# Placing every on-chip tile of a three-layer linear-attention kernel at a set distance modulo 128 bytes

## The chip, the core and the metric

The kernel runs on one core of a Trainium2 chip. The time is the device time of one execution in microseconds (us), the median of the runs named. The engines are TensorE (PE, its weight loads shown apart as PEld), VectorE (DVE), ScalarE (ACT), GpSimd (POOL) and SyncE (SP), which issues all DMAs here.

## What is computed

Three layers follow one another, for batch 8, 576 tokens, width 512 (8 heads of 64):

```python
# 1: linear attention, normalised per head
kv = einsum('bhsd,bhse->bhde', k, v)
o = einsum('bhsd,bhde->bhse', q, kv)
x = o / sqrt(mean(o*o, -1) + 1e-6) * g_norm        # heads put side by side: [B, S, 512]
# 2: gated layer
gate = sigmoid(sum_k conv_w[k] * shift(x, k))      # causal, 5 taps
x = (gate * (x @ w_val)) @ w_out
# 3: gMLP block
h = gelu_tanh(x @ w_in); u, v = h[..., :512], h[..., 512:]
v = layernorm(v) * g_ln
v = einsum('ts,bsd->btd', w_sg, v) + b_sg[:, None]
out = x + (u * v) @ w_out2
```

All inputs and the output are float32 in meaning; several weights arrive in a wider form and are converted on the chip.

## The kernel before, in words

**Products.** Every large product is done with three matmuls in the type fp32r: each operand is kept as a high part and a low part, and high x high, low x high and high x low are added in PSUM. `gemm3` (lines 212 to 220) does this for four K-tiles of 128, so it issues 12 matmuls; the stationary operand (`lhsT`, 128 x 128) changes with every matmul, the moving operand (`rhs`) has up to 512 columns. Each matmul has its own weight load, which the engine does beside the matmul before it.

**Stages, and which tile is stationary and which moving.**

- `o`, `kv`, `xT`: attention, in plain fp32 with small matmuls, and transposes.
- `val` (`Moe.val`, line 367): stationary `WV`, moving `X0h/X0l` or `X1h/X1l` (even or odd batch).
- `y` (`Moe.out`, line 388): stationary `WOh/WOl`, moving `Z`.
- `hv` (line 463, matmul in line 468): stationary `X1h/X1l`, moving `wiv`; for the last 64 tokens of two batches ("rest") the stationary tile is `kvbd0/kvbd1`.
- `hu` (line 513): stationary `wiu`, moving `X1h/X1l`. `hur` (line 561) is the same for the rest, with moving `XR`.
- `sg` (line 566, matmul in line 577): 14 matmuls of 288 columns for one piece; stationary the normalised v, which lies in `X0h`, `X0l`, `Q`, `K`, `V` and (rest) `X32`; moving the weight's high part in the tile `WV` and its low part in `G`.
- `out` (`wout2`, line 598): stationary `K/V` (which by then hold w_out2), moving `Z`; for the rest, moving `WOh`.

Of the products with 512 columns there are 384 matmuls each in `val`, `y`, `hu` and `out` and 432 in `hv`; `sg` has 896 with 288 columns; the rests have 96 with 256 columns for each of `val`, `y`, `hur` and `out`. Counts of the tags are those of the program.

**Order.** Batches 0 to 7 run through attention, `val` and `y` first, with attention of the next batch and the loading and splitting of the third layer's weights woven in by slot numbers (`Slots`, `later`, `tick`); then, batch by batch, `hu` and `sg`, then `hv` of the next batch and `out`. Intermediate results go to DRAM (`y_main`, `y_rest`) and come back. PSUM is one pool of 8 banks. The opening, up to the first `y`, is issued in an order written out by hand.

**Where tiles lie.** `sb(tag, shape)` (line 71) asks one pool for a tile. The pool lays out one place for each tag, in order of the first request, each as large as its largest user rounded up to 32 bytes per partition, behind a scratch of 16 KB for dynamic DMAs and 128 bytes of constants. A partition's tiles reach to 228,576 bytes of 229,376. All slices that the matmuls take out of a tile start at multiples of 128 bytes from its beginning (128 columns of 4 bytes are 512; 288 are 1152; 576 are 2304), so a tile's start modulo 128 bytes is that of each of its matmul operands. Worked out from the shapes, the starts modulo 128 are:

| tile | before | with the change |
|---|---|---|
| kvbd0, kvbd1 | 32 | 0 |
| WV | 64 | 0 |
| WOh, WOl | 64 | 32 |
| X32 | 64 | 0 |
| G | 0 | 0 |
| wiu | 96 | 96 |
| wiv | 96 | 64 |
| Y, Z, X0h, X0l, X1h, X1l | 96 | 0 |
| K, V | 96 | 64 |
| raw, Q, cv, T, XR | 96 | 0 |

The "distance" of a matmul is, in this document, the start of its stationary operand less the start of its moving operand, modulo 128:

| stage (columns) | stationary / moving before | distance | with the change | distance |
|---|---|---|---|---|
| val (512; rest 256) | 64 / 96 | 96 | 0 / 0 | 0 |
| y (512; rest 256) | 64 / 96 | 96 | 32 / 0 | 32 |
| hv (512) | 96 / 96 | 0 | 0 / 64 | 64 |
| hv, rest (512) | 32 / 96 | 64 | 0 / 64 | 64 |
| hu (512), hur (256) | 96 / 96 | 0 | 96 / 0 | 96 |
| out (512) | 96 / 96 | 0 | 64 / 0 | 64 |
| out, rest (256) | 96 / 64 | 32 | 64 / 32 | 32 |
| sg, X0 and Q (288) | 96 / 64 and 96 / 0 | 32 and 96 | 0 / 0 | 0 |
| sg, K and V (288) | 96 / 64 and 96 / 0 | 32 and 96 | 64 / 0 | 64 |
| sg, X32 (288) | 64 / 64 | 0 | 0 / 0 | 0 |

Of the kernel before, what the change touches and what calls it, by code (L numbers as in the profile page):

```python
# [19 lines left out]
P = 128  # L20
# [10 lines left out]
CG = math.sqrt(2.0 / math.pi)  # L31
AG = 0.044715
WC = 256

EXP_MAX = 1.875 * 2.0 ** -96
ELEMENTWISE = (mybir.EngineType.DVE, mybir.EngineType.Activation, mybir.EngineType.Pool)
# [25 lines left out]
def body(ctx, tc, qT, k, v, gcol, w_val, conv_w, w_out, w_in, g_ln, w_sgT, b_sg, w_out2, out, out_r):  # L62
    nc = tc.nc
    pool = ctx.enter_context(tc.tile_pool(name="sb", bufs=1))
# [4 lines left out]
    count = [0]  # L69

    def sb(tag, shape, dtype=F32, bufs=1):
        count[0] += 1
        return pool.tile([P] + shape, dtype, tag=tag, name=f"{tag}_{count[0]}", bufs=bufs)

    def tmp(n):

        return sb("T", [S], bufs=7)[:, :n]
# [16 lines left out]


    ident = sb("ident", [P])
    make_identity(nc, ident)
    signed = sb("GR", [2, P], F32R)
    for i, x in enumerate((1.0, -1.0)):
        nc.gpsimd.tensor_scalar(signed[:, i], ident, x, 0.0, op0=ALU.mult, op1=ALU.add)  # L100
# [34 lines left out]
    def split(src, h, l, raw=None, tmp=None, k=None, last=nc.gpsimd.tensor_tensor):  # L135
# [10 lines left out]
        def load():  # L146
            r = raw
            if r is None:
                r = sb("raw", [WC * 2], I32 if wide else F32, bufs=2)
            if not wide:  # L150
# [53 lines left out]
    def split_weight(w, src, c0, n):  # L204

        return [split(src[kt * P:(kt + 1) * P, c0 + c:c0 + c + WC], w[:, 0, kt, c:c + WC], w[:, 1, kt, c:c + WC])
                for c in range(0, n, WC) for kt in range(NK)]

# [218 lines left out]
    def w2_pieces():  # L427
        p2["kv"] = [sb(i, [5, D], F32R) for i in "KV"]
        p2["w2"] = w2 = [t[:, :NK] for t in p2["kv"]]
        return [split(w_out2[kt * P:(kt + 1) * P, c:c + WC], w2[0][:, kt, c:c + WC], w2[1][:, kt, c:c + WC])  # L430
                for c in range(0, D, WC) for kt in range(NK)]

# [230 lines left out]
    def taps():  # L663
        if conv_w.dtype == F32:
            dma(cw, conv_w)
            return lambda: None
        raw = sb("raw", [WC * 2], I32, bufs=2)[:, :2 * NK * KC]
        dma(raw, conv_w.bitcast(I32))
# [291 lines left out]
```

## Time and profile before

| what | us |
|---|---|
| median of 3 runs | 734.62 |
| lowest and highest of them | 734.25, 738.93 |
| profiled execution: span from its first to its last instruction | 733.0 |
| PE busy in it | 719.4 (98%) |
| PEld busy | 623.3 (85%) |
| DVE busy | 583.9 (80%) |
| ACT, POOL busy | 350.4 (48%), 153.3 (21%) |

The span is shorter than the median by 1.6 us, which lie around the instructions or between two executions. A matmul's recorded duration holds its whole way through the array, and consecutive matmuls overlap; what one costs in a stream is the time from its start to the start of the next, and the chain of waits shows that directly: a piece of it such as "2.72 ... x12" is 12 matmuls in a row that took 2.72 us from the first start to what follows.

### The profile page before, as it was taken

Reading aid. Unit: us, or ns where it says so; the run is one execution under the profiler, and the core shown is the slowest. Engines: PE = TensorE matmul, PEld = TensorE weight load, DVE = VectorE, ACT = ScalarE, POOL = GpSimd, SP = SyncE. Lnnn points to the kernel's source line nnn. Section 1 sums busy time; section 2 is a strip of 40 time slices with the busy share of each in tenths; the row PEclk is TensorE's granted clock in tenths of the full one; section 3 lists DMA queues with packets and bytes.
Section 4 is the critical chain, followed back from the end, with each engine's and each line's share of the span. In section 5 each row is a group of like instructions: output and inputs, shape, how many; then the busy total and the mean of one; then the engine's idle time right before and its main releaser. Section 6 shows DMA issues by size and latency. Waiting matters only on the chain.

```text
span 733.0 us, 11757 instructions
## 1 busy us (share of the span) xinstructions
PE 719.4 (98%) x4490; PEld 623.3 (85%) x4490; DVE 583.9 (80%) x1127; ACT 350.4 (48%) x667; POOL 153.3 (21%) x173
## 2 busy tenths in 40 slices
PE   8897999999999999999999999999999999999998
PEld 7686888888888888899889889888899888898897
DVE  6699979899979899699976877866866867867762
ACT  4666475566565575465533434424433424334230
POOL 1405337261627271212010000000100000100000
PEclk9999999999999999999999999999999999999999
DMA  9945253625363202533211221122240122111302
GB/s 307 352 140 202 73 193 130 223 80 195 111 223 134 87 15 86 201 97 121 68 72 58 87 101 30 58 87 59 87 158 29 59 87 62 63 63 44 101 1 86
DMA packets 56712, 81.19 MB, mean 111 GB/s; under 512 B 3664, under 2 KB 29264, under 8 KB 55632
## 3 DMA queue, kind: packets, MB, share of 16 engines
q1 hardware_dynamic: 56656, 80.45, 32.4%
q8 instruction: 35, 0.57, 0.3%
q14 instruction: 21, 0.17, 0.1%
HBM read 61.56 MB, written 18.87 MB: 110 GB/s over the span
## 4 chain that ended last, share of the span: by engine, by line
PE 86%; DVE 7%; issue 1%; POOL 1%; ACT 0%; DVEq 0%; POOLq 0%
PE sg L577 16%; PE hv L468 13%; PE out L218 13%; PE hu L218 12%; PE y L218 12%; PE val L218 11%; DVE G L349 4%; PE o L286 3%; PE xT L315 2%; PE kv L270 2%; PE hur L218 2%; DVE st L295 1%; DVE Z L381 0%; ACT Y L395 0%; DVE T L300 0%
## 5 line engine op out<-in xcount | busy, mean ns | idle before, releaser
L349 DVE SCALAR_TENSOR_TENSOR G<-X,cw,G 128x576 f32<-128x576 f32 x128 | 99.4, 826 | 6.1 <-ACT G L343 6.1
L218 PE MATMUL y<-Z,WOh 128*128 128x512 f32 (+1 forms) x320 | 98.9, 381 | 0.0
L480 POOL TENSOR_TENSOR bmv<-bmv,mhalf 128x1 f32<-128x1 f32 x36 | 21.5, 598 | 344.0 <-DVE bmv L479 344.0
L468 PE MATMUL hv<-wiv,X1h 128*128 128x512 f32 x256 | 83.1, 390 | 0.0
L218 PE MATMUL out<-Z,K 128*128 128x512 f32 x256 | 83.1, 389 | 0.0
L218 PE MATMUL hu<-X1h,wiu 128*128 128x512 f32 x256 | 79.4, 391 | 0.0
L297 POOL TENSOR_TENSOR st<-st,mhalf 128x8 f32<-128x8 f32 x40 | 70.5, 1769 | 7.4 <-DVE st L296 5.1
L218 PEld LDWEIGHTS y<-Z,WOh 128*128 128x128 f32 x320 | 57.8, 188 | 10.5
L457 ACT ACTIVATE T<-T 128x512 f32<-128x512 f32 x68 | 42.9, 631 | 44.8 <-DVE T L454 44.8
L218 PE MATMUL y<-Z,WOl 128*128 128x512 f32 (+1 forms) x160 | 58.9, 372 | 0.0
L218 PEld LDWEIGHTS out<-Z,K 128*128 128x128 f32 x256 | 48.1, 188 | 10.0
L468 PEld LDWEIGHTS hv<-wiv,X1h 128*128 128x128 f32 x256 | 47.7, 188 | 9.6 <-ACT X1h L445 0.2
L578 DVE SCALAR_TENSOR_TENSOR T<-sg,gln,WOl 128x288 f32<-128x288 f32 x64 | 32.8, 516 | 26.4 <-PE sg L577 26.2
L218 PEld LDWEIGHTS hu<-X1h,wiu 128*128 128x128 f32 x256 | 46.6, 188 | 8.3
L218 PE MATMUL hu<-X1l,wiu 128*128 128x512 f32 x128 | 50.0, 391 | 0.0
L468 PE MATMUL hv<-wiv,X1l 128*128 128x512 f32 x128 | 49.9, 390 | 0.0
L218 PE MATMUL out<-Z,V 128*128 128x512 f32 x128 | 49.8, 389 | 0.0
L589 ACT ACTIVATE Z<-T 128x512 fp32r<-128x512 f32 x32 | 20.1, 630 | 57.3 <-DVE T L588 57.3
L286 PEld LDWEIGHTS o<-kvbd,Q 128*128 128x128 f32 x320 | 40.3, 191 | 3.2 <-issue 0.7
L218 PE MATMUL val<-X0h,WV 128*128 128x512 f32 x128 | 41.4, 404 | 0.0
L286 PE MATMUL o<-kvbd,Q 128*128 128x128 f32 x320 | 40.7, 275 | 0.5 <-DMA Q<-in_qT_dram 0.5
L218 PE MATMUL val<-X1h,WV 128*128 128x512 f32 x128 | 41.2, 403 | 0.0
(174 smaller groups left out, 1709.0 us busy)
## 6 DMA issues: line engine op xcount, KB each, us to landing
Q<-in_qT_dram SPq DMA_DIRECT2D x8, 1152.0 KB, 6.0
y_main<-Y SPq DMA_DIRECT2D x8, 1024.0 KB, 3.9
raw<-y_main SPq DMA_DIRECT2D x32, 256.0 KB, 3.2
Y<-y_main SPq DMA_DIRECT2D x32, 256.0 KB, 3.9
out_dram<-Y SPq DMA_DIRECT2D x32, 256.0 KB, 2.3
K<-in_k_dram SPq DMA_DIRECT2D x7, 1024.0 KB, 5.7
V<-in_v_dram SPq DMA_DIRECT2D x7, 1024.0 KB, 9.1
raw<-in_w_in_dram SPq DMA_DIRECT2D x16, 256.0 KB, 4.7
```

The costliest lines, as they stand in the source:

```text
L218: nc.tensor.matmul(ps, lhsT=a[:, kt, msl], rhs=x[:, kt], start=(i == 0), stop=(i == 3 * NK - 1))
L270: nc.tensor.matmul(self.pk[j][h, h], lhsT=self.k[:, t, js][:, h], rhs=self.v[:, t, js][:, h], start=(t == 0), stop=(t == 4))
L286: nc.tensor.matmul(po[:, j * P:(j + 1) * P], lhsT=self.q[:, j, o:o + P], rhs=bd[:, j, :], start=True, stop=True)
L297: nc.gpsimd.tensor_tensor(st[:, 2], st[:, 1], mhalf, op=ALU.pow)
L315: nc.tensor.transpose(pt[:, j * P:(j + 1) * P], xo[:, j * P:(j + 1) * P], ident)
L349: stt(gate[:, m], x32[:, m, j:j + S], cw3[:, m, j:j + 1], gate[:, m], op0=ALU.mult, op1=ALU.add)
L457: act(w, w, AF.Tanh, scale=CG * AG)
L468: nc.tensor.matmul(ps, lhsT=a[:, kt], rhs=p2["wiv"][:, w, kt], start=(i == 0), stop=(i == 3 * NK - 1))
L480: nc.gpsimd.tensor_tensor(mv[:, 3:4], mv[:, 2:3], mhalf[:, 0:1], op=ALU.pow)
L577: nc.tensor.matmul(ps, lhsT=a[:, msl], rhs=w, start=(n == 0), stop=(n == len(mm) - 1))
L578: later(0, lambda: stt(vs[:, sl], ps, gln_s[:, m:m + 1], p2["bsg"][:, sl], op0=ALU.mult, op1=ALU.add))
L589: act(g[:, 0], x, AF.Copy)
```

## The change

Each tile's room is rounded up to 128 bytes per partition (32 words), and behind eight tags a stated number of words more is left free, which moves everything that lies behind them. The tile is asked for as a flat run of words with that padded shape and then viewed in its own shape. To have room, the scratch of the dynamic DMAs is set to 1 KB; the kernel issues all its DMAs from SP, none from POOL. With it the tiles reach to 214,656 bytes. No instruction, loop or slot is written otherwise.

```diff
+LINE = 32
+BEHIND = {"WV": 8, "WOl": -8 % LINE, "st": 0, "G": 24, "wiu": 24, "wiv": 16, "X1l": 16, "V": 16}
+
     def sb(tag, shape, dtype=F32, bufs=1):
         count[0] += 1
-        return pool.tile([P] + shape, dtype, tag=tag, name=f"{tag}_{count[0]}", bufs=bufs)
+        words = math.prod(shape)
+        room = -(-words // LINE) * LINE + BEHIND.get(tag, 0)
+        t = pool.tile([P, words], dtype, tag=tag, name=f"{tag}_{count[0]}", bufs=bufs, padded_shape=[P, room])
+        if len(shape) == 1:
+            return t
+        d = [f"d{i}" for i in range(len(shape))]
+        return t.rearrange(f"p ({' '.join(d)}) -> p {' '.join(d)}", **dict(zip(d, shape)))
...
-    nc = bacc.Bacc("TRN2", target_bir_lowering=False, num_devices=1)
+    nc = bacc.Bacc("TRN2", target_bir_lowering=False, num_devices=1, dynamic_dma_scratch_size=1024)
```

## Rows read from the trace of the kernel before

**Rows 1.** The page: busy time by engine, and the chain by line.

```profile
PE 719.4 (98%) x4490; PEld 623.3 (85%) x4490; DVE 583.9 (80%) x1127; ACT 350.4 (48%) x667; POOL 153.3 (21%) x173
...
PE sg L577 16%; PE hv L468 13%; PE out L218 13%; PE hu L218 12%; PE y L218 12%; PE val L218 11%; DVE G L349 4%; PE o L286 3%; PE xT L315 2%; PE kv L270 2%; PE hur L218 2%; DVE st L295 1%; DVE Z L381 0%; ACT Y L395 0%; DVE T L300 0%
```

**Rows 2.** Stretches: length, busy time (instructions) of each engine, granted clock, DMA share, GB/s.

```profile
core 0: us, PE busy (x) PEld busy (x) DVE busy (x) ACT busy (x) POOL busy (x), PEclk, DMA share, GB/s
0.00:18.00 18.00, 15.72 (x144) 14.28 (x146) 11.65 (x25) 8.73 (x14) 2.71 (x13) 1.00 0.92 307
18.00:30.00 12.00, 10.72 (x92) 8.65 (x87) 6.58 (x19) 6.17 (x16) 5.47 (x5) 1.00 1.02 350
30.00:66.00 36.00, 30.52 (x307) 25.30 (x305) 32.99 (x53) 24.32 (x45) 14.79 (x14) 1.00 0.69 237
66.00:333.00 267.00, 266.04 (x1777) 224.73 (x1778) 243.70 (x437) 163.31 (x315) 109.02 (x106) 1.00 0.37 129
333.00:733.00 400.00, 396.38 (x2181) 350.34 (x2179) 289.00 (x596) 147.90 (x279) 21.35 (x37) 1.00 0.22 71
```

**Rows 3.** Chain of waits in order of time, second layer: start, length, what.

```profile
133.88 1.09 ACT Y L395 x2
135.40 0.75 POOL cv L176
136.60 4.38 DVE G L349 x6
...
274.35 5.59 PE y L218 x24
279.94 11.20 PE val L218 x48
...
318.92 5.13 PE y L218 x44
```

**Rows 4.** Chain of waits in order of time, third layer.

```profile
329.94 3.12 PE hur L218 x26
...
372.63 2.72 PE hv L468 x12
375.35 5.44 PE out L218 x24
380.79 2.72 PE hu L218 x12
...
400.15 2.75 PE hu L218 x12
...
425.71 2.80 PE hv L468 x12
...
709.05 3.74 PE sg L577 x28
```

**Rows 5.** PE's instructions in order of time: start, length, operation, operands.

```profile
404.34 0.42 PE L577 MATMUL sg<-WV,X 128*128 128x288 f32 x2
404.60 0.43 PE L577 MATMUL sg<-WV,Q 128*128 128x288 f32 x2
...
406.21 0.43 PE L577 MATMUL sg<-WV,X 128*128 128x288 f32 x2
406.48 0.39 PE L468 MATMUL hv<-wiv,X1h 128*128 128x512 f32 x1
```

**Rows 6.** The same view, a rest of hv, and a rest of out.

```profile
425.55 2.96 PE L468 MATMUL hv<-wiv,kvbd 128*128 128x512 f32 x12
428.35 0.39 PE L218 MATMUL out<-Z,K 128*128 128x512 f32 x1
...
723.54 0.28 PE L218 MATMUL out<-WOh,K 128*128 128x256 f32 x1
...
727.33 0.40 PE L218 MATMUL out<-WOh,K 128*128 128x256 f32 x2
```

**Rows 7.** DVE's instructions in order of time, and the group of that line.

```profile
246.59 0.81 DVE L349 SCALAR_TENSOR_TENSOR G<-X,cw,G 128x576 f32<-128x576 f32 x1
247.32 0.29 DVE L131 TENSOR_SCALAR cv<-raw 128x256 int32<-128x256 int32 x1
247.52 1.54 DVE L349 SCALAR_TENSOR_TENSOR G<-X,cw,G 128x576 f32<-128x576 f32 x2
...
L349 DVE SCALAR_TENSOR_TENSOR G<-X,cw,G 128x576 f32<-128x576 f32 x128 | 99.4, 826 | 6.1 <-ACT G L343 6.1
```

## The prediction

> **What bounds the kernel now.** The page first. PE is busy 98% of the span, and the chain that ended last runs through PE for most of it: adding the shares of the product stages, sg 16%, hv, out 13% each, hu, y 12% each, val 11%, hur 2% make 79% [rows 1]. So the kernel is a stream of matmuls, and its time is their number times the distance in time from one start to the next. The stretches say where that isn't so: up to 66 us PE is busy 15.7 of 18, 10.7 of 12 and 30.5 of 36 us, with the DMA share at 0.92 and 1.02 in the first two and DVE at 33.0 of 36 in the third; from 66 to 333 us PE has 266.0 of 267, and after that 396.4 of 400 [rows 2]. The granted clock is 1.00 throughout, the 2.4 GHz level, so no time hangs on that. One reservation for the middle stretch: DVE has 243.7 of 267 us there, and the chain leaves PE at batch boundaries for ACT, POOL and DVE pieces such as the one from 133.9 us on [rows 2, 3].
>
> Then the chain in order of time, for the pitch of the matmuls. In 512 columns: out 5.44/24 = 226.7 ns, hv 2.72/12 = 226.7, hu between 2.72/12 and 2.75/12, say 228 [rows 4]; y 5.59/24 = 232.9, val 11.20/48 = 233.3 [rows 3]. In 256 columns: hur 3.12/26 = 120.0 [rows 4], y of the rest 5.13/44 = 116.6 [rows 3]. In 288: sg 3.74/28 = 133.6 [rows 4]. hur and out have the same distance, 0, and differ by 256 columns and 106.7 ns: 0.4167 ns a column, one cycle at 2.4 GHz. What is left over, the excess, is then 226.7 - 213.3 = 13.3 ns in 512 columns and 120.0 - 106.7 = 13.3 ns in 256. The excess is the thing this change can move. It is 19.6 for y, 20.0 for val, 15 for hu, 13.4 for out and hv (13.7 with hv's slower pieces), 13.6 for sg.
>
> Is it the operands' place that makes the difference? The telling row is the rest of hv: same stage, same line, same moving tile, same 512 columns, but stationary at 32 in place of 96, and 2.80/12 = 233.3 ns instead of 226.7 [rows 4, 6]. What other engines do doesn't explain this, and DVE's conv instructions, whose X32 operand starts at 16 different places modulo 128, take 0.81 us, or 1.54 for two in a row, with 0.826 as the mean of all 128 [rows 7].
>
> **The change part by part.** No instruction is added or removed, so the sum consists of the excess of each stage at its new place, times the stage's time on the path.
>
> *Rearranged tiles and padded shapes.* The views have the same steps as before; cost 0. Were the order of issue to change through them, the stages' slots would still be fixed by the program; I give it nothing.
>
> *Scratch of 1 KB.* No DMA is issued from POOL. 0.
>
> *DMA targets.* They move by 0 to 96 bytes modulo 128. No row has two places for one transfer. The bound on both sides: at one and the same place the first two stretches have shares of 0.92 and 1.02, so 10% of some 15 us, 1.5 us, came from other things than place; I take 0, since the opening's last half waits for DVE [rows 2], and keep +-1.5.
>
> *DVE, ACT, POOL operands.* 0, by the conv rows [rows 7]; their cover, if that fails, is PE's 98%.
>
> *Matmul operands.* Here the rows of before lack what is needed: in 512 columns they show distances 0 (226.7), 64 (233.3) and 96 (233 and 233.3), all with the moving operand at 96, and with the change it lies at 0 or 64, at a multiple of 64 bytes. That a start in the middle of 64 bytes costs more is an assumption. Rows with the moving operand at 0 or 64 exist in short matmuls only: sg 13.6 ns of excess [rows 4]; the rest of out, 32 matmuls from 723.54 to 727.33 us, 118.4 ns or 11.8 of excess [rows 6]; the two matmuls of sg on X32, with both operands at 64, 0.26 us and 0.27 us for a pair, 130 and 135 ns or 10 and 15 of excess [rows 5]. The bounds: no excess at all below, and 22.7 (236 ns, 2.7 above the slowest row) above. I take 11.8, the one of these rows whose operands are all from the same loop as y, val, hu and out.
>
> The sum, stage time on the path (share of 733.0) times the change of pitch: y 88 x 7.8/232.9 = 2.9; val 81 x 8.2/233.3 = 2.8; hu 88 x 3.2/228 = 1.2; hv 95 x 1.9/227 = 0.8; out 95 x 1.6/226.7 = 0.7; sg 117 x 1.8/133.6 = 1.6; hur and other rests 0.3. Together 10.3 us. It counts fully only if DVE keeps up between 66 and 333 us: 5.7 us of it fall there, which takes DVE from 91% to 93%; what is late next there is the conv chain at the batch boundaries [rows 3].
>
> The profiled span of 733.0 becomes 722.7; the median lies 1.6 above the span, so 724.3, rounded to 724.
>
> Weighed against the Trainium skill: its page "SBUF — State Buffer", section "Who interferes with whom", gives PE two independent read ports, one for the moving operand and one for weight loads, and says that PE never waits on anyone. By that rule the places can't matter and the time stays at 734.6; the trace disagrees as far as the rest of hv goes (233.3 against 226.7), which is why the rule is only a rival here.
>
> "TensorE: Matmul & The Clock Gate", section "Back-to-back issue gap", has N/2.4 + 2.5 ns for one matmul after another; with that as the pitch of all stages (215.8, 122.5, 109.2 ns) an estimate by this page is some 38 us less, 697. No row here comes near 2.5 ns of excess.
>
> **The rivals.**
>
> *Distance alone decides (slower).* The price follows the distance and not the 64-byte start. Then val goes from 96 to 0 and gains 81 x 6.6/233.3 = 2.3; but hu goes from 0 to 96 and loses 88 x 5.2/228 = 2.0, hv and out go from 0 to 64 and lose 95 x 6.4/227 = 2.7 and 95 x 6.6/226.7 = 2.8; y at distance 32 and sg are left as they are. Net +5.2: 739.8. For it: every 512-column row of before obeys it. Against: in 256 columns the order is the other way round, 120.0 at distance 0 and 116.6 at 96. It decides from the point at which hv's and out's pitch is 233 after the change.
>
> *All at their worst.* Every 512-column stage at 236 ns and sg at its slowest pair, 138: y and val +2.1, hu +3.1, hv and out +7.8, sg +3.9, in all +17: 751. Nothing in the rows asks for it.
>
> *A shorter wait is hit.* The 13.3 ns at distance 0 are the same in 256 and 512 columns, which looks like a fixed wait per matmul, 32 cycles. If a well-placed start needs half of it, 6.7 ns, then y, val 5.0 and 4.6, hu 3.2, hv, out 2.9 each, sg 6.0, rests 0.8 are saved, 25 us: 709.
>
> *Nothing happens.* The places matter less than other things in each stage, gains and losses cancel: 734.6. For it: excesses of all stages lie within 12 to 20 ns whatever the place, and an offset of 64 bytes costs 6.6 ns at most, 3% of the pitch.
>
> **How the numbers follow.** A measurement of this kernel can tell about 1%, 7.3 us, from no change; faster is below 727.3, slower above 742.0. The forecast has 0.47; by itself it holds from 716 (excess 9) to 730 (excess 14), of which 0.37 lies below 727.3 and 0.10 above. The shorter wait 0.10, all faster. Nothing 0.20, all same. Distance alone 0.15, of which 0.12 same and 0.03 slower, since y may lose too. All at their worst 0.08, slower. Faster 0.47, same 0.42, slower 0.11. The range goes from 708, just below the shorter wait, to 740, just above distance alone; left out are the worst case and the tails.
>
> **What would show it.** In the chain of the changed kernel, twelve matmuls in 512 columns should take 2.70 us (225 ns) in every stage, and 28 of sg 3.69. If val's twelve take 2.72 while hv's and out's take 2.80, distance alone is right. If twelve take 2.64 (220 ns), the shorter wait is. If y and val get shorter and the end doesn't move with them, DVE's conv chain has taken over between 66 and 333 us; the pieces of ACT, POOL and DVE in the chain would then be longer than before. The opening should end its PE-poor part at 66 us as before, within 1.5. The forecast is wrong if any 512-column stage stands at 230 ns or more.

## The result and the profile after

The changed kernel takes 740.38 us (median of 6 runs, 739.96 to 742.41), the kernel before 735.05 in the same series: ratio 1.0072, 95% interval 1.0052 to 1.0092. It is slower by 0.7%, 5.3 us; 724 was forecast, with a range of 708 to 740.

The page of the changed kernel has the same number of instructions on every engine and, within 0.6 us, the same busy time on all but two of them: PE has 727.0 us instead of 719.4, PEld 624.6 instead of 623.3 [rows 1]. All lines are nine further down than before. Busy time by engine, and the chain by line:

```profile
PE 727.0 (98%) x4490; PEld 624.6 (84%) x4490; DVE 583.8 (79%) x1127; ACT 350.4 (47%) x667; POOL 153.9 (21%) x173
...
PE sg L586 16%; PE out L227 14%; PE hv L477 14%; PE hu L227 12%; PE y L227 12%; PE val L227 11%; DVE G L358 4%; PE o L295 3%; PE xT L324 2%; PE kv L279 2%; PE hur L227 2%; DVE st L304 1%; DVE Z L390 0%; ACT Y L404 0%; DVE T L309 0%
```

The chain of waits in order of time (start, length, what) has the same pieces as before, so each can be held against its own [rows 3, 4]:

```profile
65.59 1.11 PE xT L324 x4
66.70 3.73 PE y L227 x12
...
275.22 5.61 PE y L227 x24
280.83 11.20 PE val L227 x48
...
329.73 4.78 PE hur L227 x41
...
374.55 2.79 PE hv L477 x12
377.34 5.60 PE out L227 x24
382.94 2.80 PE hu L227 x12
...
398.78 3.71 PE sg L586 x28
...
428.58 2.79 PE hv L477 x12
```

Divide by the counts: out 233.3 ns (226.7 before), hv 232.5 (226.7), hu 233.3 (226.7 to 229), y 233.8 (232.9), val 233.3 (as before; its shorter pieces take 2.78 to 2.79 for twelve, before 2.80), sg 132.5 (133.6), hur 116.6 (120.0). With the shares of the path that the prediction used: hu 88 x 5.3/228 = 2.0, hv 95 x 5.8/227 = 2.4, out 95 x 6.6/226.7 = 2.8, y 0.3, and back come sg 117 x 1.1/133.6 = 1.0 and hur 0.4. That is +6.1 against 5.3 measured, but it is rougher than it looks: out's share holds its rest of 256 columns too, and sg's and hur's other pieces differ by less than these rows (the second hur takes 5.65 us for 48, before 5.75). Summed over the two traces, each matmul from its start to the start of the next, hu costs 1.7 us more, hv 2.2, out 2.4, y 0.5 (without the clock's dip below), and the rests of val, y and out together 0.7; back come sg 0.6, val 0.4 and hur 0.2. That is +6.3. The rest of hv, the last row, is unchanged at 2.79.

The spans differ by more than the medians, 739.9 against 733.0. One reason stands in the first two chain rows, four `xT` in 1.11 us and twelve `y` in 3.73, where the kernel before has

```profile
66.22 0.66 PE xT L315 x4
66.87 2.81 PE y L218 x12
```

Stretches of the changed kernel, the last three columns being granted clock, DMA share and GB/s, show why:

```profile
core 0: us, PE busy (x) PEld busy (x) DVE busy (x) ACT busy (x) POOL busy (x), PEclk, DMA share, GB/s
60.00:64.00 4.00, 2.73 (x14) 1.93 (x12) 3.08 (x7) 2.31 (x5) 4.00 (x3) 1.00 1.05 388
64.00:66.00 2.00, 0.41 (x2) 0.41 (x3) 2.00 (x4) 1.13 (x2) 0.76 (x1) 0.80 0.67 216
66.00:68.00 2.00, 2.00 (x8) 1.71 (x7) 2.00 (x6) 1.26 (x3) 0.00 (x0) 0.50 0.03 9
```

After PE was busy for 2.73 of 4 us and 0.41 of 2, the granted clock stood at 0.50, the 1.2 GHz level, for the next two us. That costs (3.73 - 2.81) + (1.11 - 0.66) = 1.4 us here. The profiled execution of before has no dip, with PE busy for 3.35 of the same 4 us and 0.00 of the same 2. These 1.4 and the 6.3 of the pitches, less 0.6 by which the opening is shorter (first `y` at 59.24 us, before at 59.86), make 7.1; the spans differ by 6.9.

The dip is not bound to the new places: the kernel of the first experiment, which takes the time of the kernel before, has it in its profile too (last row of experiment 1). Whether it falls as often in both kernels is open. Five of the six executions of the changed kernel have a mean granted clock of 0.998 and one has 0.997; of the 54 of the kernel before that went with the experiments, 16 have 1.000 and took 734.2 to 735.5 us, 12 have 0.998 and took 735.3 to 737.3, and the others have 0.994 to 0.997 and took 734.1 to 737.6. So up to 1.4 of the measured 5.3 us may be the dip and not the pitches, and whether the places have a part in how often it falls is not shown.

### The profile page after: what moved, and what is told of

Same layout as the page of the kernel before. It is cut to its first block, busy times and chain, and to the rows that moved or that the text cites. A ratio compares the mean times of both kernels' runs of the same rounds, so it can differ in the third digit from the quotient of the medians.

```text
span 739.9 us, 11757 instructions
## 1 busy us (share of the span) xinstructions
PE 727.0 (98%) x4490; PEld 624.6 (84%) x4490; DVE 583.8 (79%) x1127; ACT 350.4 (47%) x667; POOL 153.9 (21%) x173
## 4 chain that ended last, share of the span: by engine, by line
PE 86%; DVE 7%; issue 1%; POOL 1%; ACT 0%; DVEq 0%; POOLq 0%
PE sg L586 16%; PE out L227 14%; PE hv L477 14%; PE hu L227 12%; PE y L227 12%; PE val L227 11%; DVE G L358 4%; PE o L295 3%; PE xT L324 2%; PE kv L279 2%; PE hur L227 2%; DVE st L304 1%; DVE Z L390 0%; ACT Y L404 0%; DVE T L309 0%
## 5 line engine op out<-in xcount | busy, mean ns | idle before, releaser
L227 PEld LDWEIGHTS out<-Z,K 128*128 128x128 f32 x256 | 47.9, 187 | 11.8
```

Source lines behind the costliest of these rows:

```text
L227: nc.tensor.matmul(ps, lhsT=a[:, kt, msl], rhs=x[:, kt], start=(i == 0), stop=(i == 3 * NK - 1))
```

## The experiments

Theory A is the rival "distance alone": the price of a matmul follows its distance modulo 128. Theory B takes a longer period, 256 or 512 bytes. Theory C says that what counted before was not the distance but the common start at 96. Diffs are against the changed kernel; numbers in `BEHIND` are words.

**1. Scratch and flat views alone.**

```diff
-        room = -(-words // LINE) * LINE + BEHIND.get(tag, 0)
-        t = pool.tile([P, words], dtype, tag=tag, name=f"{tag}_{count[0]}", bufs=bufs, padded_shape=[P, room])
+        t = pool.tile([P, words], dtype, tag=tag, name=f"{tag}_{count[0]}", bufs=bufs)
```

> The change without its rounding and its extra words: scratch of 1 KB and flat tiles viewed in their shape. Every tile moves by 15,360 bytes, a multiple of 512, so all distances and starts modulo 512 are those of before. If only the operands' places make the difference: same time as before within 0.2%, twelve matmuls of out 2.72 us, of val 2.80. If the smaller scratch or the flat views cost something, the change's 0.7% or a part of it stands here.

Measured: 734.83 us against 734.89, ratio 0.9999 (0.9986 to 1.0012). The chain of this kernel:

```profile
281.37 11.20 PE val L223 x48
...
376.75 5.44 PE out L223 x24
```

Pitches as before: the two parts that the prediction priced at 0 cost 0, and everything comes from the places. Its stretch from 66 to 68 us shows the clock's dip:

```profile
66.00:68.00 2.00, 1.70 (x6) 1.58 (x7) 2.00 (x5) 0.55 (x1) 0.00 (x0) 0.50 0.08 22
```

**2. All at distance 0, at two common starts.**

```diff
-BEHIND = {"WV": 8, "WOl": -8 % LINE, "st": 0, "G": 24, "wiu": 24, "wiv": 16, "X1l": 16, "V": 16}
+BEHIND = {"mhalf": 64, "cw": 32, "X32": 96, "st": 96, "T": 64}    # all large tiles at 0 modulo 512
+BEHIND = {"mhalf": 24, "cw": 32, "X32": 96, "st": 96, "T": 64}    # the other kernel: at 352
```

> All large tiles start at 0 modulo 512, so every product has the distance 0 modulo 512. Theory A, distance modulo 128 alone: 12 matmuls of 512 columns take 2.72 us in val, y, hu, hv and out, the time is that of before less 2.3 (val) and 2.3 (y), 730.4. Theory B, distance modulo 512: the same 2.72 and 730.4. Theory C, the common start of 96 modulo 128 is what counts and not the distance: 2.78 to 2.80 in all stages, 740 or more.

> All large tiles start at 352 modulo 512 (96 modulo 128), where before has Z, X, K, V, wiu and wiv; WV and WO move there. All three theories: 2.72 us for twelve matmuls of each stage, 730.4. A and B expect the same time as with all tiles at 0, theory C some 10 us less.

Measured: 0.9965 of the kernel before (0.9951 to 0.9979) at 0 and 0.9958 (0.9943 to 0.9973) at 352, some 732 us. Both beat both kernels. The chain with all at 0:

```profile
117.28 2.74 PE val L227 x12
...
150.39 2.77 PE val L227 x12
...
273.78 5.50 PE y L227 x24
279.28 10.88 PE val L227 x48
...
374.38 5.44 PE out L227 x24
379.82 2.72 PE hu L227 x12
```

and with all at 352:

```profile
274.68 5.49 PE y L227 x24
280.17 10.88 PE val L227 x48
...
375.28 5.44 PE out L227 x24
```

The common start makes no difference, 5.44 and 5.44, 10.88 and 10.88. Theory C falls, and with it the assumption that a moving operand should start at a multiple of 64 bytes: 352 isn't one, 0 is. The time gains 2.6 to 3.1 us instead of the 4.6 expected. The val rows show one part of the rest: 48 in a row take 226.7 ns each, but twelve between other work take 228 to 231. Another part is DVE, whose conv chain the prediction had named. What PE waited for between 70 and 333 us (total us, times, longest), in the kernel before and with all at 0:

```profile
PE xT L315 <- DVE T L300: 0.7, 2, 0.4
...
PE xT L324 <- DVE T L309: 1.5, 4, 0.6
```

With all at 352 it is 1.5 us in four waits as well, and DVE's conv line is 7% of the whole chain in both, 4% before. A third part is the rests of val and y: 256 columns at distance 0 take about 120 ns, before about 117, 0.5 us in all.

Theory A has a hole here too: in the changed kernel val has the distance 0 modulo 128 and took 233.3 ns; here, at 0 modulo 512, the same 48 take 226.7.

**3. Which period: a different distance for each stage.**

```diff
+BEHIND = {"mhalf": 64, "cw": 64, "WV": 32, "WOl": 64, "X32": 96, "st": 72, "wiu": 96, "wiv": 24, "X1l": 48, "raw": 40, "T": 64}
```

> Moving operands of the 512-column stages at 0 modulo 512 (hv's at 416), and a different distance modulo 512 for each stage: val 128, y 256, hu 32, hv 96, out 192. Theory A: val and y have distance 0 modulo 128 and take 2.72 us for twelve, out has 64 and takes 2.80. Theory B: all five take 2.78 to 2.81. If the period is 256: y alone takes 2.72. Nothing is known of 32 and 96 (hu, hv).

The chain:

```profile
272.98 5.50 PE y L227 x24
278.48 11.15 PE val L227 x48
...
374.75 5.50 PE out L227 x24
380.25 2.80 PE hu L227 x12
...
406.25 5.61 PE hv L477 x24
```

y at 256 takes 5.50 for 24, what it took at 0; val at 128 takes 232.3 ns. So the period is 256 bytes: A falls, and B in its form with 256 stands. In 256 bytes the changed kernel's distances are val 128, y 160, hu 96, hv and out 64; of before val and y 224, hu, hv, out 0. A single execution of this kernel took 736.83 us.

**4. Only out moved, in the kernel before.** Is the pitch the whole effect on the end?

```diff
+BEHIND = {"mhalf": 104, "cw": 72, "X32": 112, "st": 120, "X1l": 16, "V": 112}    # before's places modulo 512, but K, V 64 further on
```

> The kernel before with K and V alone moved by 64 bytes, so that only out's distance goes from 0 to 64 (and its rest's from 32 to 96). If the pitch of the matmuls is the whole effect: twelve matmuls of out take 2.80 us instead of 2.72, all other stages as before, and the time is 384 x 6.4 ns = 2.5 us over that of before, ratio 1.0034. If the end is set by something else in the third layer, the pitch changes and the time doesn't.

Measured: ratio 1.0033 (1.0021 to 1.0046), 737.97 against 735.43 us, +2.5. The chain:

```profile
374.76 2.75 PE hv L477 x12
377.51 5.60 PE out L227 x24
383.11 2.75 PE hu L227 x12
```

out goes to 233.3 ns, its neighbours in time only from 2.72 to 2.75 us, and the end moves by the price of 384 matmuls. K and V are also the stationary tiles of out's rest and of 128 of the 896 matmuls of sg; summed over the trace, hu and hv take 0.2 and 0.3 us more and sg 0.3 less, so out's own 2.4 us are what is left.

**5. The map in steps of 16 bytes.**

```diff
+BEHIND = {"mhalf": 64, "cw": 80, "WV": 8, "WOh": 128, "WOl": 72, "X32": 96, "st": 80, "wiu": 96, "wiv": 112, "X1l": 56, "K": 128, "V": 72, "T": 64}
+FRONT = {"WOh": 4, "WOl": 4, "wiu": 4, "wiv": 4, "K": 4, "V": 4}
...
-        t = pool.tile([P, words], dtype, tag=tag, name=f"{tag}_{count[0]}", bufs=bufs, padded_shape=[P, room])
+        f = FRONT.get(tag, 0)
+        t = pool.tile([P, f + words], dtype, tag=tag, name=f"{tag}_{count[0]}", bufs=bufs, padded_shape=[P, room])
+        t = t[:, f:]
```

The second kernel differs in `BEHIND` alone.

> A map in finer steps: distance modulo 256 of val 192, y 240, hu 208, hv 176, out 240; moving operands at 0 modulo 256 (hv's at 80). If a period of 256 bytes with a shift of 32 bytes and more away from 0 being bad is all there is: about 233 ns for all but val, which takes 229 as out did at 192. If distances just below 0 are good too: y and out, both at 240, stand together at 227 or less. Other stages with one and the same distance must agree in either case.

> The second half of the map: val 224, y 16, hu 240, hv 16, out 208. If the distance modulo 256 is the variable and not the stage: val 233 as before at the same distance, hu the value that y and out have at 240 in the run sent with this one, out the value that hu has there at 208, and y and hv, both at 16, agree with each other.

All the distances seen, each from a chain piece of 12 to 48 matmuls of 512 columns:

| distance modulo 256 | stage: ns from one start to the next |
|---|---|
| 0 | out 226.7, val 226.7, y 229.2 |
| 16 | y 233.3, hv 235.8 and 227.5 |
| 32 | hu 233.3 |
| 64 | out 233.3, hv 232.5 |
| 96 | hu 233.3, hv 233.8 |
| 128 | val 232.3 to 233.3 |
| 160 | y 233.8 |
| 176 | hv 231.3 |
| 192 | out 229.2, val 228.8 |
| 208 | hu 231.7, out 233.3 |
| 224 | val 233.1, y 232.9 |
| 240 | out 227.9, hu 229.2, y 229.2 |

Three of the rows behind it, out at 240 from the first kernel:

```profile
373.83 5.47 PE out L230 x24
```

hv at 16 and out at 208 from the second:

```profile
378.41 5.60 PE out L230 x24
...
409.89 5.66 PE hv L480 x24
...
423.91 2.73 PE hv L480 x12
```

Stages that share a distance agree within 1.6 ns, but for 0 and 16. At 0 it is y, which alternates with other work, that stands 2.5 ns higher. At 16 hv itself has more than one pitch in one and the same kernel: 235.8 ns in the pieces of 24 behind sg, 227.5 in the twelves between two pieces of out (the last row; seven such twelves stand in the chain), with all operands at the same distance. So the distance does not settle the pitch alone; what the stream follows has a part in it. Of the places seen none is better than 0; 240 and 192 come near, and apart from those twelves everything else is 4 to 9 ns dearer. 48, 80, 112 and 144 were not seen, and sg is left out because its two halves start 1152 bytes apart, so that its distance modulo 256 changes by 128 from one half to the other. Single executions of the two kernels took 734.76 and 740.69 us.

**6. The change with three stages put back.**

```diff
+BEHIND = {"mhalf": 64, "cw": 64, "WV": 8, "WOl": 88, "X32": 96, "st": 96, "T": 64}    # hu, hv, out at 0; val 128, y 160 modulo 256
```

> The change with the third layer's three products put back to distance 0 modulo 256 (wiu, wiv, K and V at the same place as their partners), while val and y keep the distances that the change gives them modulo 256 (128 and 160). If hu, hv and out are where the change loses its time: 384 x 5.0 (hu, 233.6 to 228.6), 432 x 6.0 (hv) and 384 x 6.6 ns (out) come back, 7.0 us, and the time is 733.4, ratio 0.998 to before. If the loss sits in the second layer or in the opening, the time stays near 740.

Measured: 732.96 us, ratio 0.9977 (0.9966 to 0.9987); 733.4 and 0.998 were expected. The chain:

```profile
273.37 5.60 PE y L227 x24
278.97 11.20 PE val L227 x48
...
374.53 5.44 PE out L227 x24
379.97 2.72 PE hu L227 x12
```

val and y stand as the change leaves them, hu, hv and out at distance 0 as before, and the loss is gone. It ends 1.7 us below the kernel before. Part of that is sg, whose 28 take 3.69 us here:

```profile
395.61 3.69 PE sg L586 x28
```

By this row that would be 117 x 1.8/133.6 = 1.6 us; summed over the trace it is 1.1. Another part is the rest of hv, which stands at 0 here and stood at 64 before (48 matmuls, 0.3 us).

**7. The rests at 192.** In 256 columns the best place is another: in the third experiment both out and its rest stood at 192 modulo 256. The last batch's 48 matmuls of 512 columns and 48 of 256 are one piece of the chain; in the third experiment's kernel it is

```profile
715.01 16.44 PE out L227 x96
```

and in the one with all at 0

```profile
710.59 16.67 PE out L227 x96
```

Less 48 x 229.2 and 48 x 226.7 ns for the long ones, the short ones took 113 and 121 ns each (the 121 holds the end of the program; the other 48 of the same stage take 119.8). So XR, the moving tile of two other rests, is put at 192 from its partners:

```diff
+BEHIND = {"mhalf": 64, "cw": 32, "X32": 96, "st": 96, "T": 48}    # all at 0, XR at 64
```

> All large tiles at distance 0 as in the run with all at 0, and XR alone moved by 64 bytes, so that the two products with XR as moving operand and 256 columns (hur and the rest of val) have the distance 192. By the map, 192 modulo 256 gives 113.3 to 115.9 ns in 256 columns and 0 gives 119.8: 2 x 96 x about 5 ns, 1 us less than with all at 0, ratio 0.995 to before. If those rests are hidden behind other work, no change against all at 0.

Measured: 730.93 us, ratio 0.9945 (0.9932 to 0.9959), the fastest of all the kernels here. The chain, hur:

```profile
325.61 4.66 PE hur L227 x41
...
531.74 5.66 PE hur L227 x48
```

113.7 ns each in the first piece and 117.9 in the second, at the same places, against 120.0 at distance 0 [rows 4]: here too one distance has two pitches. Summed over the trace, hur and the rest of val take 0.5 us less than with all at 0, half of the 1 us expected. The intervals of this run and of the one with all at 0 overlap, so the 1 us between their medians is not shown by the times, and the pitch accounts for half of it.

## Why the prediction was wrong

**What bounds the kernel: right.** The time is matmuls times pitch. Moving out alone added 2.5 us for 384 matmuls of 6.6 ns [experiment 4], and putting three stages back returned what their counts and pitches said, 732.96 us for the 733.4 expected [experiment 6].

**Scratch, views, order: right, 0** [experiment 1]. **DMA targets and the other engines: right, 0 within what can be seen.** The chain's first y starts at 66.70 us, before at 66.87, the opening's end moves by 0.6 us, less than the 1.5 allowed, and the engines' busy times are the same.

**The step that failed is the excess at the new places.** I said that a start in the middle of 64 bytes costs more was an assumption, and then took 11.8 ns for every stage from the rest of out, a row of 256 columns. Both were wrong. The start makes no difference by itself [experiment 2]; and 256 and 512 columns have different maps: at 192 the excess is 7 to 11 ns in 256 columns (113.7 and 117.9, less 106.7) and 229.2 - 213.3 = 16 in 512; at 0 it is 13.3 in both. In place of 11.8 the runs show 19 to 21 ns for hu, hv, out, y and val (all five above the 230 ns that the prediction gave as its sign of being wrong), which is what the kernel before already showed for 512 columns away from distance 0. The row of the rest of hv, 233.3 ns at distance 64 in the same stage, length and moving tile, was the nearest row for hv and out, and I called it telling and then priced by another one.

**Distance alone, given 0.15, was the rival that came true, by a partly wrong reckoning.** It gave 739.8, and 740.4 was measured. Its terms for hu (2.0), hv (2.7) and out (2.8) are each some 0.4 above what the trace shows (1.7, 2.2 and 2.4). Its gain for val of 2.3 did not come, because the period is 256 bytes and val stood at 128 in it, not at 0 (val gave 0.4); and it left out sg and hur, which gave 0.8 back, the rests, which cost 0.7, and the dip of the clock. That the total came so near is luck. Its weak point, that 256 columns have the order the other way round, was a true observation and no argument against it.

**A shorter wait (0.10) and nothing (0.20)** are refuted for these places: no stage came to 220 ns, and the ratio's interval excludes 1. "Nothing" rested on the Trainium skill's page "SBUF — State Buffer", section "Who interferes with whom", by which PE's two read ports are independent and PE waits for nobody. The trace disagrees: with only the stationary tile of out moved, 226.7 became 233.3 ns.

**DVE as a brake between 66 and 333 us** could not show in the changed kernel, since y and val did not get shorter there: PE waits for DVE 0.7 us behind 70 us, as before. Where they did get shorter the reservation was right: the waits are 1.5 us [experiment 2].

## What to carry to other kernels

In a stream of fp32r matmuls with new weights each time, let the stationary and the moving operand start at the same place modulo 256 bytes: here 226.7 ns against about 233 for 512 columns, and 3 us in all by moving tiles. Expect less than pitch times count where another engine is nearly as busy: here PE's waits for DVE took up 0.8 us of the gain. Price a place by a row of the same length, from more than one piece of the chain, and before relying on a period check it with one run that gives each stage another distance. Where a difference of under 1% is read from two profiled spans, look first for a stretch with another granted clock.

## What the runs showed that was not expected

- The pitch depends on the distance of the two operands modulo 256 bytes, in steps as small as 16: 226.7 at 0, 235.8 at 16 behind sg. Moving both together from 0 to 352 changed nothing.
- The best distance depends on the length: of those seen, in 512 columns 0, in 256 columns 192 (113.7 to 117.9 against 120.0 ns).
- One distance can have two pitches: hur at 192 takes 113.7 and 117.9 ns in one kernel, hv at 16 takes 227.5 and 235.8. At distance 0, too, it matters what the stream follows: with all at 0, twelve hu take 2.72 us behind out and mostly 2.73 to 2.75 behind sg, and val takes 226.7 ns in the 48 behind y and 228 to 231 in most twelves between attention's matmuls.
- What inside the chip makes the distance matter was not found; the runs settle that the distance decides most of the price in 512 columns, not the cause, nor what chooses between two pitches at one distance.
